# Attention followed by two feed-forward stages: another order for the start, the division by row sums through a wide copy, and 24 products of ones

## The chip, the cores and the metric

The kernel runs on one core of a Trainium2 chip. The metric is the device time of one execution in microseconds. The engines of the core are TensorE (PE; its weight loads are listed as PEld and overlap with its products), VectorE (DVE), ScalarE (ACT), GpSimd (POOL) and SyncE (SP), which issues the transfers. Each engine takes its own instructions in order, and an instruction that waits holds up all that stand behind it on that engine.

## The reference

```python
def _attn_ref(q, k, v, g_q, g_k):                  # 4 x 12 heads x 448 x 64
    def rmsnorm(x, g):
        rms = np.sqrt(np.mean(x * x, axis=-1, keepdims=True) + 1e-06)
        return x / rms * g
    q_n, k_n = (rmsnorm(q, g_q), rmsnorm(k, g_k))
    scores = np.matmul(q_n, k_n.transpose(0, 1, 3, 2)) / np.sqrt(64)
    scores = scores - np.max(scores, axis=-1, keepdims=True)
    attn = np.exp(scores)
    attn = attn / (np.sum(attn, axis=-1, keepdims=True) + 1e-09)
    return np.matmul(attn, v)
...
x = attn_out.transpose(0, 2, 1, 3).reshape(1792, 768)
h = x @ w_in                                       # 768 -> 2048
x = np.maximum(0.01 * h, h) @ w_out                # 2048 -> 768
...
for e in range(8):                                 # each token goes to its best expert
    h = np.maximum(x[mask] @ w1[e], 0.0)
    out[mask] = gate_w[mask, None] * eom[mask, e, None] * (h @ w2[e])
```

## The kernel before

The kernel has three stages: attention, a feed-forward stage (`FirstMoe`), and a second one with eight experts. The change is in the attention alone.

**Tiling.** The 48 heads are taken as 24 pairs (`PAIRS`). Both heads of a pair lie side by side on the 128 partitions, 64 each. The 448 rows of a head are NC = 4 chunks of CP = 112 rows.

**One pair, step by step.** `load` fetches q and k into `qk` (112 x 1024, L177), `load_v` fetches v (L183). `square` squares both on ACT (L192) and adds up each row's 64 squares on DVE (L193) into `ms`. `roots` makes the inverse root of `ms` in nine small DVE steps (L213 to L222); `together` lays the `ms` of two pairs side by side, so that one chain of roots serves both. `norm` multiplies q and k by it (L240, on POOL, for the first pair half on DVE). `turn_k` and `turn_q` transpose the normed chunks on PE (L248) and write them as a high part on ACT (`kh` L267, `qh` L256) and a low part on DVE (`kl` L268, `ql` L63). `top` makes the scores of one chunk (L275), and DVE takes their maximum per row (`md`, L277). `row` transposes the four maxima (L282), and ACT copies them to `mx` (L284). `probs` makes the scores again, transposed, from high and low parts with the maximum taken off (L298, eight products), and ACT takes exp of them (L300, `p` or `pr`). POOL adds the four chunks' exponentials into `pr` (L313). `values` multiplies them with v into `av` (L309).

**The division.** `sums` adds up the exponentials over the partitions with products against `ones_mat` (L321), ACT copies them to `sp` (L325), `back` turns them with four small products (L332), and DVE takes the reciprocals `r`, 112 x 8 (L335). `spread` lays them out in the shape of `av`: eight products of `r`, broadcast to 64 columns, with `ident` (L342; the trace counts 16, two for each float32 product). `scale` copies that to `rt` on ACT (L348) and multiplies `av` with it on DVE (L350). `store` writes the result as `xTh` (ACT, L355) and a low part (DVE, L63).

**The order.** In the attention the order on PE, DVE, ACT and POOL is as written out by hand in `pieces`: a prologue for pair 0, `begin(i)` for the pairs 0 to 2, `steady(i)` for the pairs 3 to 22. While pair i makes its `probs`, the next one (`one`) makes its tops and the one before (`prev`) is divided and stored. The last pair and `FirstMoe` are placed by a scheduler. From pair 8 on, weights of `FirstMoe` are fetched and unpacked beside the attention (`decode`, L580 to L588, on ACT, DVE and POOL), in every second pair, and in some late ones where the scheduler puts more. In PSUM the transposes share two buffers (`tr`), the scores of `probs` have one (`sc`), the tops one (`tp`), `av` two. `FirstMoe` makes its first products at L627 to L629 (`mo`).

## Time and profile before

| what | value |
|---|---|
| three runs, median | 1232.29 us |
| three runs, lowest and highest | 1229.84 and 1232.62 us |
| the profiled execution | 1230.19 us |
| its span in the profile | 1228.4 us |
| PE busy | 1158.2 us (94%) |
| DVE busy | 775.5 us (63%) |
| ACT busy | 500.3 us (41%) |
| POOL busy | 456.4 us (37%) |

The span is the time from the first to the last instruction; 1.8 us of the execution lie around it. The shares are means over three stages with different limits, so a change in one stage is read from the rows of that stage: how long an engine was idle before an instruction, and which engine released it. The attention with its handover to `FirstMoe` takes the first 322 us or so, `FirstMoe` ends near 870, and the experts take the rest.

### The profile page before, as it was taken

To read this page: it belongs to the slowest core of one execution; us is meant where nothing else is said; L and a number is where in the kernel's file an instruction comes from. 1 tells how busy PE (TensorE), PEld (TensorE's weight loads), DVE (VectorE), ACT (ScalarE), POOL (GpSimd) and SP (SyncE) were. 2 spreads that over 40 slices of the span, in tenths; PEclk is the share of its full clock that TensorE was granted. 3 is DMA by queue.
4 is the path that set the end of the run, shared out by engine and by line. 5 is a ranking of instruction groups with operands and counts; after the bars stand their busy time and mean duration, and the time that the engine had idled before them with its cause. 6 is when DMAs were issued, how large, how long until landed. Compare 5 with 4: busy or idle time off the path is not lost.

```text
span 1228.4 us, 19094 instructions
## 1 busy us (share of the span) xinstructions
PE 1158.2 (94%) x6988; PEld 930.8 (76%) x6988; DVE 775.5 (63%) x1326; ACT 500.3 (41%) x791; POOL 456.4 (37%) x301
## 2 busy tenths in 40 slices
PE   4899999989899899999999999999799999999997
PEld 2455555545568788888888889888598988998986
DVE  6777888876627786858585854446745179215446
ACT  2566666655335422222222321132344167225444
POOL 1667767757324331313232220000414047113334
PEclk9999999989899999999999999999699999999999
DMA  5212222111102220202020200343357059413456
GB/s 149 60 47 61 68 80 73 50 29 29 46 13 77 78 77 26 78 26 78 26 78 26 78 26 1 133 118 88 117 199 249 24 197 354 153 47 125 172 201 227
DMA packets 68081, 116.28 MB, mean 95 GB/s; under 512 B 6780, under 2 KB 45948, under 8 KB 67968
## 3 DMA queue, kind: packets, MB, share of 16 engines
q1 hardware_dynamic: 64528, 103.87, 26.6%
q0 software_dynamic: 3120, 11.02, 2.6%
q8 instruction: 57, 0.93, 0.3%
q14 instruction: 56, 0.46, 0.1%
q10 hardware_dynamic: 320, 0.00, 0.0%
HBM read 106.61 MB, written 12.58 MB: 97 GB/s over the span
## 4 chain that ended last, share of the span: by engine, by line
PE 77%; DVE 10%; issue 5%; ACT 3%; DMA 2%; POOL 2%; ACTq 0%; DVEq 0%; POOLq 0%; SPq 0%
PE mo L627 6%; PE mo L628 6%; PE mo L629 6%; PE sc L298 6%; PE av L309 6%; PE mp L646 6%; PE mp L647 5%; PE mp L648 5%; PE ph L990 4%; PE ph L989 3%; PE ph L988 3%; PE py L1006 3%; PE py L1004 3%; PE py L1005 3%; DVE w1l L63 2%
## 5 line engine op out<-in xcount | busy, mean ns | idle before, releaser
L654 DVE TENSOR_TENSOR ysum<-mp,ysum 128x448 f32<-128x448 f32 x168 | 103.8, 621 | 111.1 <-PE mp L648 109.5
L313 POOL TENSOR_TENSOR pr<-pr,p 112x896 f32<-112x896 f32 x72 | 153.2, 2128 | 49.6 <-ACT p L300 35.4
L627 PE MATMUL mo<-xTh,w0h 128*128 128x448 f32 x384 | 142.8, 372 | 13.2 <-DVE g L634 9.4
L646 PE MATMUL mp<-gh,w1h 128*128 128x448 f32 x384 | 144.4, 377 | 1.4 <-ACT ysum L652 0.7
L628 PE MATMUL mo<-xTl,w0h 128*128 128x448 f32 x384 | 141.8, 369 | 0.2 <-DVE xTl L63 0.2
L647 PE MATMUL mp<-gl,w1h 128*128 128x448 f32 x384 | 141.8, 369 | 0.0
L629 PE MATMUL mo<-xTh,w0l 128*128 128x448 f32 x384 | 141.4, 368 | 0.0
L648 PE MATMUL mp<-gh,w1l 128*128 128x448 f32 x384 | 140.4, 368 | 0.0
L588 POOL TENSOR_TENSOR raw<-raw,top 128x384 f32<-128x384 f32 x64 | 65.2, 1020 | 191.1 <-DVE raw L586 166.7
L277 DVE TENSOR_REDUCE md<-tp 112x2 f32<-112x896 f32 x96 | 104.4, 1088 | 17.7 <-PE tp L275 17.4
L1004 PE MATMUL py<-w2h,hT 128*128 128x384 f32 x288 | 99.7, 346 | 0.0
L63 POOL TENSOR_TENSOR w1l<-r,w1h 128x1024 fp32r<-128x1024 f32 x17 | 42.9, 2528 | 149.4 <-ACT w1h L952 75.1
L1006 PE MATMUL py<-w2l,hT 128*128 128x384 f32 x288 | 96.8, 336 | 0.0
L1005 PE MATMUL py<-w2h,hL 128*128 128x384 f32 x288 | 96.5, 335 | 0.0
L63 DVE TENSOR_TENSOR hL<-pt,hT 128x512 fp32r<-128x512 f32 x36 | 24.8, 689 | 106.3 <-ACTq L1014 59.3
L627 PEld LDWEIGHTS mo<-xTh,w0h 128*128 128x128 f32 x384 | 72.5, 189 | 24.1 <-DVE g L634 12.1
L990 PE MATMUL ph<-w1l,xgh 128*128 128x512 f32 x216 | 86.4, 400 | 4.2 <-DVE w1l L63 4.2
L988 PE MATMUL ph<-w1h,xgh 128*128 128x512 f32 x216 | 86.7, 402 | 0.0
L989 PE MATMUL ph<-w1h,xgl 128*128 128x512 f32 x216 | 85.8, 397 | 0.0
L63 POOL TENSOR_TENSOR w1l<-raw,w1h 128x768 fp32r<-128x768 f32 x16 | 31.4, 1984 | 141.7 <-ACT w1h L596 141.7
L646 PEld LDWEIGHTS mp<-gh,w1h 128*128 128x128 f32 x384 | 72.4, 189 | 13.0 <-DVE ysum L654 4.1
L300 ACT ACTIVATE p<-sc 112x896 f32<-112x896 f32 x72 | 66.0, 917 | 39.8 <-PE sc L298 35.6
(199 smaller groups left out, 2499.8 us busy)
## 6 DMA issues: line engine op xcount, KB each, us to landing
r<-in_moe_w_dram SPq DMA_DIRECT2D x27, 1024.0 KB, 5.5
r<-in_moe_w_dram SPq DMA_DIRECT2D x36, 768.0 KB, 7.3
wd<-in_moe_w_in_dram SPq DMA_DIRECT2D x32, 384.0 KB, 3.3
wd<-in_moe_w_out_dram SPq DMA_DIRECT2D x32, 384.0 KB, 3.1
qk<-in_q_dram SPq DMA_DIRECT2D x24, 224.0 KB, 3.0
qk<-in_k_dram SPq DMA_DIRECT2D x24, 224.0 KB, 3.2
vv<-in_v_dram SPq DMA_DIRECT2D x24, 224.0 KB, 2.8
x2d<-xn SPq DMA_DIRECT2D x24, 224.0 KB, 2.9
```

Of the source, the lines that this page charges most:

```text
L63: engine.tensor_tensor(dst, src, hi.bitcast(F32), ALU.subtract)
L313: nc.gpsimd.tensor_tensor(st["pr"][:CP], st["pr"][:CP], p, ALU.add)
L627: nc.tensor.matmul(ph, wh_[:, c], xh, start=(c == 0), stop=False)
L628: nc.tensor.matmul(ph, wh_[:, c], xl, start=False, stop=False)
L629: nc.tensor.matmul(ph, wl_[:, c], xh, start=False, stop=(c == KD - 1))
L646: nc.tensor.matmul(py, hi[:, sl], gh, start=(j == 0), stop=False)
L647: nc.tensor.matmul(py, hi[:, sl], gl, start=False, stop=False)
L648: nc.tensor.matmul(py, lo[:, sl], gh, start=False, stop=(j == GF - 1))
L990: nc.tensor.matmul(ph[n], xh[:, c], w1l[:, c, s_], start=False, stop=(c == K1 - 1))
L1004: nc.tensor.matmul(py[n], hT[:, c], w2h[:, c, s_], start=(c == 0), stop=False)
L1005: nc.tensor.matmul(py[n], hL[:, c], w2h[:, c, s_], start=False, stop=False)
L1006: nc.tensor.matmul(py[n], hT[:, c], w2l[:, c, s_], start=False, stop=(c == K2 - 1))
```

## The change

**Division.** A new step `widen` copies `r` on ACT to `wide` (112 x 512: each reciprocal 64 times). `spread` then transposes `wide` chunk by chunk, four transposes in place of eight float32 products. On PE `spread` moves from ahead of `probs` of chunk 3 to behind it, behind the next pair's first top and behind `row(one)`; `scale` moves with it. `square` is split, so that ACT squares before it widens and DVE's sum stands where it stood.

**Start.** The first two pairs are squared together, get one chain of roots (112 x 32), and pair 0 is normed wholly on DVE, k first, pair 1 on POOL. The transposes of pair 1 go in between the tops of pair 0, and these tops take turns between two buffers. The small product `gg` (L111, now `join_constants`) comes behind the sums of squares. One chain of roots moves from pair 0 to pair 1.

**Products of ones.** At the start PE makes WARM = 24 products of `ones_mat` with itself (128 x 128), which need no transfer, and ACT reads one column of the result (`seen`).

```diff
+    def join_constants():
         nc.vector.scalar_tensor_tensor(gg, gg, ROOT ** -2, gk, ALU.mult, ALU.mult)
...
-                (nc.vector if t and st is self.first else nc.gpsimd).tensor_tensor(
+                (nc.vector if st is self.first else nc.gpsimd).tensor_tensor(
...
-        def top(self, st, c):
-
-            sc = self.tp()
+        def top(self, st, c, other=0):
+
+            sc = self.sc() if other else self.tp()
...
+        def widen(self, st):
+
+            wide = self.pool.tile([CP, NC, 2, DH], F32, name="wide", bufs=1)
+            nc.scalar.activation(
+                wide, st["r"].rearrange("p j c -> p c j").unsqueeze(3).to_broadcast([CP, NC, 2, DH]), AF.Copy)
+            st["wide"] = wide
+
         def spread(self, st):
-            tr = st["tr"] = self.tr()
-            for c in range(NC):
-                for j in range(2):
-                    nc.tensor.matmul(
-                        tr[j * DH:(j + 1) * DH, c * CP:(c + 1) * CP],
-                        st["r"][:, j, c:c + 1].to_broadcast([CP, DH]), ident[:CP, :CP], start=True, stop=True)
+            st["tr"] = self.turned_of(st["wide"].rearrange("p c j d -> p c (j d)"))
...
-                st = sts[0]
-                self.together(sts[:1])
+                st, one = sts[:2]
+                self.together(sts[:2])
                 self.square(st)
-                self.roots(sts[:1])
-                self.norm(st)
+                self.square(one)
+                join_constants()
+                self.roots(sts[:2])
+                self.norm(st, (1, 0))
+                self.norm(one, (1, 0))
+                warm = self.sc()
+                for _ in range(WARM):
+                    nc.tensor.matmul(warm[:, 0, :P], ones_mat, ones_mat, start=True, stop=True)
+                seen = self.pool.tile([P, 1], F32, name="seen", bufs=1)
+                nc.scalar.activation(seen, warm[:, 0, :1], AF.Copy)
                 self.turn_k(st, 0)
                 self.turn_q(st, 0)
-                self.together(sts[1:2])
                 for c in range(NC):
-                    self.top(st, c)
+                    self.top(st, c, c % 2)
                     if c == 1:
-                        self.square(sts[1])
-                self.roots(sts[1:2])
+                        self.turn_k(one, 1, apart=True)
+                        self.turn_q(one, 1, apart=True)
                 self.row(st)
-                self.norm(sts[1])
+                one["klow"]()
+                one["low"]()
...
             self.back(prev)
+            if at(i + 6):
+                self.square(at(i + 6), (0,))
+            self.widen(prev)
             self.values(cur, 1)
-            self.spread(prev)
...
-            self.scale(prev)
             self.probs(cur, 3)
             if two:
                 self.top(two, 0)
+            self.row(one)
+            self.spread(prev)
             self.values(cur, 2)
+            self.scale(prev)
             self.store(prev)
-            self.row(one)
```

In the three places below a row is an instruction with its output, its inputs, its shape and its count.

PE at the start, before; `tr<-ident,qn` are the transposes of q and k, `md_137` the maxima of pair 0:

```order
L248 MATMUL tr<-ident,qn 128x112 x8
L275 MATMUL tp<-kh,qh 112x448 x8
L282 MATMUL tr<-ident,md_137 128x112 x4
L298 MATMUL sc<-qh,kh 112x448 x2
L298 MATMUL sc<-ql,kh 112x448 x2
```

PE at the start, after:

```order
L390 MATMUL sc<-ones_mat 128x128 x24
L254 MATMUL tr<-ident,qn 128x112 x8
L283 MATMUL tp<-kh,qh 112x448 x2
L283 MATMUL sc<-kh,qh 112x448 x2
L254 MATMUL tr<-ident,qn 128x112 x8
L283 MATMUL tp<-kh,qh 112x448 x2
L283 MATMUL sc<-kh,qh 112x448 x2
L290 MATMUL tr<-ident,md_137 128x112 x4
L306 MATMUL sc<-qh,kh 112x448 x2
L306 MATMUL sc<-ql,kh 112x448 x2
```

The ones come first, and the eight transposes of pair 1 now stand between the tops of pair 0 (in the kernel before they follow its first `probs`).

PE in a steady pair, before, from `back` to the next pair's first transposes:

```order
L332 MATMUL av<-ident,sp 112x4 x2
L309 MATMUL av<-p,vv 64x448 x2
L342 MATMUL tr<-ident,r 64x112 x8
L298 MATMUL sc<-qh,kh 112x448 x2
L298 MATMUL sc<-ql,kh 112x448 x2
L298 MATMUL sc<-qh,kl 112x448 x2
L298 MATMUL sc<-mx,mask 112x448 x2
L275 MATMUL tp<-kh,qh 112x448 x2
L309 MATMUL av<-p,vv 64x448 x2
L282 MATMUL tr<-ident,md_139 128x112 x4
L248 MATMUL tr<-ident,qn 128x112 x4
```

PE in the same steady pair, after:

```order
L340 MATMUL av<-ident,sp 112x4 x2
L317 MATMUL av<-p,vv 64x448 x2
L306 MATMUL sc<-qh,kh 112x448 x2
L306 MATMUL sc<-ql,kh 112x448 x2
L306 MATMUL sc<-qh,kl 112x448 x2
L306 MATMUL sc<-mx,mask 112x448 x2
L283 MATMUL tp<-kh,qh 112x448 x2
L290 MATMUL tr<-ident,md_139 128x112 x4
L254 MATMUL tr<-ident,wide 128x112 x4
L317 MATMUL av<-p,vv 64x448 x2
L254 MATMUL tr<-ident,qn 128x112 x4
```

The eight products on `r` are gone from their place, and four transposes of `wide` stand behind `probs`, top and row.

ACT in the same steady pair, before, from the exp of chunk 2 (the first row) to the next pair's first exp (the last):

```order
L300 ACTIVATE p<-sc 112x896
L192 ACTIVATE sq<-qk 112x1024
L348 ACTIVATE rt<-tr 128x448
L300 ACTIVATE p<-sc 112x896
L355 ACTIVATE xTh_114<-av 128x448
L284 ACTIVATE mx<-tr 128x448
L267 ACTIVATE kh<-tr,gg 128x448
L300 ACTIVATE pr_133<-sc 112x896
```

ACT in the same steady pair, after:

```order
L308 ACTIVATE p<-sc 112x896
L197 ACTIVATE sq<-qk 112x1024
L349 ACTIVATE wide<-r 112x512
L308 ACTIVATE p<-sc 112x896
L292 ACTIVATE mx<-tr 128x448
L358 ACTIVATE rt<-tr 128x448
L365 ACTIVATE xTh_114<-av 128x448
L273 ACTIVATE kh<-tr,gg 128x448
L308 ACTIVATE pr_133<-sc 112x896
```

The copy to `wide` stands ahead of the exp of chunk 3, and `rt` moved behind that exp.

## Rows read from the trace of the kernel before

**Rows 1.** Stretches: us from and to, length, each engine's busy time, TensorE's granted clock

```profile
core 0: us, PE busy (x) PEld busy (x) DVE busy (x) ACT busy (x) POOL busy (x), PEclk, DMA share, GB/s
69.00:257.00 188.00, 186.12 (x1633) 105.49 (x1630) 153.39 (x262) 122.70 (x182) 134.71 (x85) 1.00 0.21 61
257.00:322.00 65.00, 54.53 (x421) 29.63 (x422) 43.18 (x61) 28.85 (x44) 40.34 (x24) 0.89 0.12 34
367.00:870.00 503.00, 487.60 (x2554) 432.46 (x2552) 335.17 (x663) 149.86 (x265) 117.58 (x86) 0.99 0.22 64
```

**Rows 2.** Time line at the start: start, us, engine, line, operation, [idle before <-releaser]

```profile
4.14 0.31 SPq L177 DMA_DIRECT2D qk<-in_k_dram  x1
...
7.06 1.27 DVE L193 TENSOR_REDUCE ms<-sq 112x8 f32<-112x512 f32 x2
...
11.09 1.82 PE L248 MATMUL tr<-ident,qn 112*128 112x112 f32 x8 [11.09 <-DVE qn L240]
...
14.29 1.09 DVE L277 TENSOR_REDUCE md<-tp 112x2 f32<-112x896 f32 x1
```

**Rows 3.** The page's transfers: issues, KB each, median us from issue to landing

```profile
qk<-in_k_dram SPq DMA_DIRECT2D x24, 224.0 KB, 3.2
```

**Rows 4.** Time line, PE, first three pairs

```profile
21.37 0.45 PE L282 MATMUL tr<-ident,md 112*128 112x112 f32 x1 [0.44 <-DVE md L277]
...
25.24 1.76 PE L248 MATMUL tr<-ident,qn 112*128 112x112 f32 x8 [1.66 <-POOL qn L240]
...
37.61 0.32 PE L282 MATMUL tr<-ident,md 112*128 112x112 f32 x1 [0.58 <-DVE md L277]
...
55.12 0.67 PE L282 MATMUL tr<-ident,md 112*128 112x112 f32 x4
```

**Rows 5.** Time line, the roots and the stall of the second pair

```profile
38.72 1.03 DVE L213 TENSOR_SCALAR ms<-ms 112x32 f32<-112x32 f32 x1
...
39.85 2.08 DVE L214 TENSOR_SCALAR y<-ms 112x32 int32<-112x32 int32 x1
...
45.69 0.45 PE L275 MATMUL tp<-kh,qh 64*112 64x448 f32 x2 [3.42 <-DVE md L277]
```

**Rows 6.** Time line, PE in a steady pair

```profile
112.56 0.59 PE L321 MATMUL tr<-pr,ones_mat 113*32 113x112 f32 x16
...
115.66 0.99 PE L342 MATMUL tr<-ident,r 112*64 112x112 f32 x16
...
116.57 0.46 PE L298 MATMUL sc<-qh,kh 64*112 64x448 f32 x2
...
118.68 0.60 PE L282 MATMUL tr<-ident,md 112*128 112x112 f32 x4
...
119.12 0.55 PE L248 MATMUL tr<-ident,qn 112*128 112x112 f32 x4
...
124.33 0.59 PE L321 MATMUL tr<-pr,ones_mat 113*32 113x112 f32 x16
```

**Rows 7.** Groups by line and shape: count, busy us, mean ns, idle before

```profile
L192 ACT ACTIVATE sq<-qk 112x512 f32<-112x512 f32 x2 | 1.1, 612 | 0.0
```

**Rows 8.** Time line, ACT in the same steady pair

```profile
115.06 1.05 ACT L192 ACTIVATE sq<-qk 112x1024 f32<-112x1024 f32 x1
...
117.74 0.92 ACT L300 ACTIVATE p<-sc 112x896 f32<-112x896 f32 x1 [0.44 <-PE sc L298]
```

**Rows 9.** Time line, PE in the pair of the first late stall

```profile
262.72 1.76 PE L342 MATMUL tr<-ident,r 112*64 112x112 f32 x16 [3.97 <-DVE r L335]
...
269.21 0.46 PE L298 MATMUL sc<-qh,kh 64*112 64x448 f32 x2
```

**Rows 10.** Time line before the first feed-forward stage

```profile
304.30 1.74 DVE L581 TENSOR_SCALAR top<-wd 128x384 int32<-128x384 int32 x1 [2.31 <-DMA wd<-in_moe_w_out_dram]
...
310.34 0.71 PE L275 MATMUL tp<-kh,qh 64*112 64x448 f32 x2 [2.22 <-DVE md L277]
...
321.42 0.47 PE L627 MATMUL mo<-xTh,w0h 128*128 128x448 f32 x1 [1.86 <-DVE md L277]
```

More of the change, by code (lines that the diff above doesn't have):

```diff
@@ L184, in load_v, with square @@
                 st["v"], v[b, 2 * hp:2 * hp + 2].rearrange("h (p c) d -> p h (c d)", c=NC))
-        def square(self, st):
+        def square(self, st, parts=(0, 1)):
             n = 4 * NC
             flat = st["qk"].rearrange("p t h (c d) -> p (t h c) d", d=DH)
-            sq = self.early.tile([CP, n, DH], F32, name="sq", bufs=2)
+            if 0 in parts:
+                st["sq"] = self.early.tile([CP, n, DH], F32, name="sq", bufs=2)
+            sq = st["sq"]
             for h in (slice(0, n // 2), slice(n // 2, n)) if st is self.first else (slice(0, n),):
-                nc.scalar.activation(sq[:, h], flat[:, h], AF.Square, scale=DH ** -0.5)
-                nc.vector.tensor_reduce(st["ms"][:, h], sq[:, h], AX.X, ALU.add)
+                if 0 in parts:
+                    nc.scalar.activation(sq[:, h], flat[:, h], AF.Square, scale=DH ** -0.5)
+                if 1 in parts:
+                    nc.vector.tensor_reduce(st["ms"][:, h], sq[:, h], AX.X, ALU.add)
         def together(self, sts):
@@ L260, in turn_q, with turn_k @@
             st.update(qh=qh, ql=ql, md=self.MX[i % len(self.MX)], pr=self.PR[i % len(self.PR)])
-        def turn_k(self, st, i):
+        def turn_k(self, st, i, apart=False):
             kh = self.pool.tile([P, S], F32R, name="kh", bufs=3)
@@ L267, in turn_k @@
             nc.scalar.activation(kh, tk, AF.Copy, scale=gg)
-            nc.vector.scalar_tensor_tensor(kl, tk, gg, kh.bitcast(F32), ALU.mult, ALU.subtract)
+            st["klow"] = lambda: nc.vector.scalar_tensor_tensor(kl, tk, gg, kh.bitcast(F32), ALU.mult, ALU.subtract)
+            if not apart:
+                st["klow"]()
             st.update(kh=kh, kl=kl)
-        def top(self, st, c):
-            sc = self.tp()
+        def top(self, st, c, other=0):
+            sc = self.sc() if other else self.tp()
             for j, rows in enumerate(HALVES):
@@ L397, in pieces @@
                     self.back(sts[n - 2])
+                    self.widen(sts[n - 2])
                 elif op == "C":
@@ L406, in pieces @@
             self.back(last)
+            self.widen(last)
             yield
@@ L417, in begin @@
                 todo = [[("square", 2)], [("roots", 2, 3), ("norm", 2)], [("square", 3)],
-                        [("square", 4), ("roots", 3, 5)]]
+                        [("square", 4)]]
             elif i == 1:
-                todo = [[("norm", 3)], [("square", 5)], [("norm", 4)], []]
+                todo = [[("roots", 3, 5), ("norm", 3)], [("square", 5)], [("norm", 4)], []]
             else:
                 todo = [[("square", 6)], [("roots", 5, 7), ("norm", 5)], [("norm", 6)], []]
-            for lo, hi in {0: ((2, 3), (3, 5)), 1: ((5, 7),)}.get(i, ()):
+            for lo, hi in {0: ((3, 5),), 1: ((5, 7),)}.get(i, ()):
                 self.together(sts[lo:hi])
             for c in range(NC):
-                if c == 3 and prev:
-                    self.scale(prev)
                 self.probs(cur, c)
-                if i == 0 and c == 0:
-                    self.turn_k(one, 1)
-                    self.turn_q(one, 1)
                 self.top(one, c)
@@ L434, in begin @@
                     self.back(prev)
+                    self.widen(prev)
+                elif c == 3 and prev:
+                    self.spread(prev)
+                    self.scale(prev)
                 if c:
@@ L440, in begin @@
                     self.sums(prev)
-                elif c == 2 and prev:
-                    self.spread(prev)
                 elif c == 3 and prev:
@@ L503, in steady @@
             self.back(prev)
+            if at(i + 6):
+                self.square(at(i + 6), (0,))
+            self.widen(prev)
             self.values(cur, 1)
-            self.spread(prev)
             if not begun:
@@ L511, in steady @@
             if at(i + 6):
-                self.square(at(i + 6))
+                self.square(at(i + 6), (1,))
             yield
-            self.scale(prev)
             self.probs(cur, 3)
@@ L518, in steady @@
                 self.top(two, 0)
+            self.row(one)
+            self.spread(prev)
             self.values(cur, 2)
+            self.scale(prev)
             self.store(prev)
-            self.row(one)
             if three:
@@ L529, in attention_moe_moe2 @@
     FROM = 3
+    WARM = 24
     ORDER = "P0 S P1 C V0 P2 V1 P3 V2 V3".split()
```

1 line of the change is left out of this document (added).

## The prediction

> **What bounds the kernel now.** I read the busy times by stretch first, then the time line of the stretches in which TensorE is idle. In the steady attention TensorE works 186.1 of 188 us, and in the first feed-forward stage 487.6 of 503 [rows 1]. In both it is the bound: whatever else is made faster there gives nothing, and what is taken off TensorE comes back in full until another engine is late. VectorE, the next, has 153.4 of the 188. Between 257 and 322 TensorE works 54.5 of 65 us, at a granted clock of 0.89. There it waits, so the reader must look at what ends each wait. The start is the third kind: TensorE's first instruction comes at 11.09 [rows 2], and three marks divide what follows, the transposes of the maxima that close the prologue, the first and the second pair, at 21.37, 37.61 and 55.12 [rows 4]. These are 10.3, 16.2 and 17.5 us, while a steady pair takes 124.33 - 112.56 = 11.77 [rows 6].
>
> The clock at the start is read from durations: eight transposes take 1.82 at 11.09 and 1.76 at 25.24 [rows 2, 4], where four take 0.55 later on [rows 6], so TensorE is still at its lower level of 1.2 GHz, after a start in which it did nothing.
>
> **The steady pairs.** On TensorE the spread of the reciprocals takes from 115.66 to 116.57, 0.91 us. The transposes that replace it have the form of those at 118.68, which take 0.44 until the next begin [rows 6]. That is 0.47 less in each pair; I take 0.44, for a change of form between the products. ScalarE pays for it with one copy of 112x512. The nearest row is the square of that shape, 0.61 us [rows 7]; the copy reads a broadcast of 112x8, which no row shows, so I bound it by half of that and by the full 112x1024 square, 1.05 [rows 8], and take 0.61, the same output. It is hidden: the square ends at 116.11, r is out before 115.66 (where TensorE takes it now), so the copy ends near 116.7. The exp behind it starts now at 117.74; without the spread ahead of its products it could start at 116.8. TensorE comes to the new transposes only behind four more groups of products and one of transposes, near 118.6, so it doesn't wait for the copy. On ScalarE the copy to rt now stands between the exp and the next pair's kh, and the next exp, now at 120.70 and then wanted at 120.25, comes out within about 0.1 us of that: a tie, not a reserve. VectorE has (188 - 153.4)/188 of its time free, enough for a pair that is 4% shorter. There are 18 pairs from the 4th to the 23rd without a stall: 18 x 0.44 = 7.9, between 6 and 8.5.
>
> **The start.** The chain to the first transposes gets longer. The second pair's k is issued at 4.14 and needs 3.2 [rows 2, 3], so it is there at 7.3; a square of 1.05 [rows 8] ends at 8.4, its sums (two halves take 1.27, [rows 2]) at 9.6, where the sums now end at 8.33. From there to the first transposes it is 2.76 now, and the roots of twice the columns cost a little more (0.15, an estimate). First transposes: 11.09 + 1.3 + 0.15, about 12.5. From there the first maximum is taken 3.2 later now (11.09 to 14.29, at the lower clock). With two buffers for the tops the four maxima follow each other at 1.09, with one low part of about 0.7 before the row: 12.5 + 3.2 + 4 x 1.09 + 0.7 = 20.8, and 20.1 with a fast clock, against 21.37 now. The prologue gives about 0.9.
>
> The gain is behind it. The first pair then has no transposes of the second in it, and VectorE's four maxima, three sums of squares and two small chains set it: 4 x 1.09 + 3 x 1.27 + about 2, some 10.2 us; with TensorE's part at a lower clock up to 13. So its mark comes at 31 to 33.7 (37.61 now). In the second pair the stall of 3.42 at 45.69 goes [rows 5], with its roots one step earlier; but two root steps there took 1.03 and 2.08 us beside GpSimd's additions, more together than the whole chain and norm of pair 0 (2.76), and the changed kernel puts a chain of roots in the same pair. I take 12.9 for it, a steady pair and 1.1 of such delay. Its mark then comes at 44 to 46.6 instead of 55.12: 8.5 to 11. I take 9, near the slow end, because the clock may be slow again (below).
>
> What the Trainium skill says of this delay (SBUF — State Buffer, "SBUF: two separate sides") is that VectorE and GpSimd share a port pair as an exclusive lock, held for a whole instruction. The two rows agree in size with that, since a GpSimd addition lasts about as long as the longer of them. By the page the delay would come back wherever roots meet additions, which is what I assume.
>
> **The products of ones** are 24 with two passes each. Sixteen passes of 112 columns take 1.76 slow and 0.99 fast [rows 6, 9], so 48 of 128 columns take 6.0 or 3.4, and up to 10.6 if a pass costs what a transpose costs at the slow level (1.82 / 8, [rows 2]). They need no transfer, so they lie within the wait for the first transposes and cost nothing. They end between 5 and 12, so TensorE may be idle again for up to 7 us before it begins at 12.5. The rows tell what idling does: after 3.97 us the spread at 262.72 took 1.76 in place of 0.99 [rows 9]. So I count no gain in the first transposes themselves. The term above holds without the ones.
>
> **The late stalls.** In the pair around 262 TensorE stands 3.97 us for the reciprocals, because they queue on VectorE behind unpacking of weights, and then runs the spread, the products, and all up to 269.21 partly at the lower clock [rows 9]. In the new order the products of chunk 3, a top and the row stand ahead of the spread, so they run inside the wait. What is left behind r is the copy, the spread and one group of values: the next pair's products could begin at about 265.0 instead of 269.21, 4.2 with the 0.45 of a clean pair in it. The price of the move: the exp of chunk 3 now stands behind the copy, which waits for r, and the POOL additions behind that exp. I take 3.0, between 0.45 and 4.3.
>
> Between 297 and 322 VectorE waits for weights from memory (2.31 at 304.30), TensorE for VectorE (2.22 at 310.34, 1.86 at 321.42) [rows 10]. No edit makes those transfers earlier in themselves, but TensorE has more to do in the wait. I take 3.0, between 0 and 6. The last pair gets the copy in its chain and loses 0.47 on TensorE: nothing. Behind that the two feed-forward stages are unchanged and TensorE's, so what is gained ahead of them stays.
>
> **Sum.** 9 + 7.9 + 3.0 + 3.0 = 22.9 off the profiled execution's 1230.2 gives 1207.3. That execution lies 2.1 below the median of the three runs, 1232.3, from which the same sum gives 1209.4. I say 1208.
>
> **Rivals.**
> Slow clock at the start: the gap behind the ones returns TensorE to 1.2 GHz, and it stays there through the first pair, whose products then bound it. For it speaks the row at 262.72, against it that a pair without gaps came back within some 5 us there (at 269.21 a group takes 0.46 again). The start then gives 5 or 6 instead of 9: 1212. The Trainium skill (TensorE: Matmul & The Clock Gate, "Part 4: PE-mode transpose") adds that transposes don't count as busy for the clock in the same way as products; by it the sixteen transposes of the new prologue would prolong this. The row at 25.24, slow after 14 us of transposes and tops, doesn't speak against it.
>
> The stalls stay: VectorE is as late for weights as before, and the exp behind the copy makes the GpSimd additions, and with them the sums, late. Then the last two terms give 0.9 instead of 6: 1213.
>
> The tie on ScalarE is lost: each pair's next exp comes 0.4 late and takes the saving of the steady pairs. The sum is 15 instead of 22.9: 1216.
>
> Slower than before: the broadcast copy is far dearer than a square of its shape. The exp behind it must be over when the next pair's products need their buffer, near 119.1, so start by 118.2; from 116.11 the copy may take 2.1 us without harm. Past that each microsecond costs one in each of some 21 pairs. The gain of 22.9 and 3.7 more, over 21 pairs, is 1.3: from 3.4 us on the kernel is slower by more than 0.3%, and at 4.0 it takes about 1247 (1207.3 + 21 x 1.9). For it speaks only that no row shows such a read; against it the 0.61 of the same output.
>
> That the change doesn't do what it says holds for the ones: if they end early, the first transposes take 1.8 as before. It costs nothing in my sum.
>
> **Chances and range.** My forecast 0.62, slow clock 0.15, stalls that stay 0.12, the lost tie 0.06, the dear copy 0.05, of which 0.02 within 0.3% of before (3.7 us, what a measurement of this kernel can tell from none) and 0.03 beyond. All but the last are faster: 0.95. The range runs from the upper ends of the terms (11 + 8.5 + 4.3 + 6 = 29.8, 1200 to 1202; I cut it to 1200, since they will hardly all come together) to the lost tie, 1216.
>
> **What will show it.** The first transposes near 12.5, and their duration, 1.8 or 1.0; the transposes of the maxima near 20.5, 32.5 and 45.5; four transposes of the wide tile in 0.44, a steady period of 11.3 us, and the copy at 0.6 with no wait of an exp behind it; in the pair of 262 no long wait for r on TensorE with work queued behind; the first product of the feed-forward stage near 298.5. I am wrong if the steady period stays at 11.7, if the second mark comes after 35, or if the wait before the first feed-forward product grows by what was gained ahead of it.

## The result, and the profile after

The changed kernel takes 1214.5 us (median of four runs, 1211.78 to 1217.62) where the kernel before takes 1232.39: a ratio of 0.986, with a 95% interval of 0.9833 to 0.9887, or 17.9 us less. The profiled execution took 1211.78 with a span of 1210.0, the shortest of the four; against the 1228.4 of before that is 18.4. The forecast was 1208, with a range of 1200 to 1216.

The place of the gain is read from marks in both time lines: the start of the sums of a pair (the 16 products with `ones_mat`, L321 before and L329 after), the first product of `FirstMoe`, the start of its last `mp` product (L646 before, L668 after), and the end.

| mark | before | after | earlier by |
|---|---|---|---|
| sums of the 4th pair | 89.02 | 81.30 | 7.7 |
| sums of the 18th pair | 255.29 | 242.87 | 12.4 |
| sums of the 19th pair (first late stall) | 273.96 | 259.31 | 14.65 |
| sums of the 21st pair | 297.49 | 282.09 | 15.4 |
| first product of `FirstMoe` | 321.42 | 303.71 | 17.7 |
| last `mp` product | 860.4 | 841.8 | 18.6 |
| end | 1228.4 | 1210.0 | 18.4 |

So the four terms of the sum came out as 7.7 for the start (9 forecast), 5.45 for the steady pairs (7.9; 4.70 up to the 18th pair and 0.75 in two more), 2.2 for the first late stall (3.0) and 2.3 for the handover to `FirstMoe` (3.0). The other 0.7 appears only behind the first product of `FirstMoe`.

The steady pair that answers to [rows 6] and [rows 8], after, on TensorE and ScalarE:

```profile
115.49 0.59 PE L329 MATMUL tr<-pr,ones_mat 113*32 113x112 f32 x16
...
117.99 1.05 ACT L197 ACTIVATE sq<-qk 112x1024 f32<-112x1024 f32 x1
118.33 0.20 DVE L343 RECIPROCAL r<-av 112x8 f32<-112x8 f32 x1
...
118.94 0.62 ACT L349 ACTIVATE wide<-r 112x512 f32<-112x512 f32 x1
...
119.75 0.92 ACT L308 ACTIVATE p<-sc 112x896 f32<-112x896 f32 x1 [0.20 <-PE sc L306]
...
120.22 0.55 PE L254 MATMUL tr<-ident,wide 112*128 112x112 f32 x4
...
120.70 0.97 PE L317 MATMUL av<-p,vv 112*64 112x448 f32 x4
...
121.60 0.60 PE L254 MATMUL tr<-ident,qn 112*128 112x112 f32 x4
...
122.14 0.46 PE L306 MATMUL sc<-qh,kh 64*112 64x448 f32 x2
...
123.25 0.92 ACT L308 ACTIVATE pr<-sc 112x896 f32<-112x896 f32 x1
...
126.88 0.59 PE L329 MATMUL tr<-pr,ones_mat 113*32 113x112 f32 x16
```

From sums to sums it is 11.39 instead of 11.77. The transposes of `wide` run from 120.22 to 120.70, 0.48 where the eight products took 0.91, without a wait; the copy ends at 119.56, and the exp behind it waits only for its products. But the transposes of `qn`, which stood right behind other transposes, now stand behind products and hold TensorE from 121.60 to 122.14, 0.54 where it was 0.48. 0.91 - 0.48 - 0.06 = 0.37, and 0.38 is measured.

The start, after, answering to [rows 2] and [rows 4]:

```profile
1.14 8.12 PE L390 MATMUL sc<-ones_mat 128*128 128x128 f32 x48 [1.14 <-DVE ones_mat L70]
...
8.46 1.06 ACT L197 ACTIVATE sq<-qk 112x1024 f32<-112x1024 f32 x1 [2.27 <-DMA qk<-in_k_dram]
...
12.81 2.14 DVE L246 TENSOR_TENSOR qn<-qk,y 112x512 f32<-112x512 f32 x2
12.86 2.99 POOL L246 TENSOR_TENSOR qn<-qk,y 112x512 f32<-112x512 f32 x2 [10.01 <-DVE y L228]
13.65 0.98 PE L254 MATMUL tr<-ident,qn 112*128 112x112 f32 x4 [4.40 <-DVE qn L246]
...
22.93 0.98 PE L290 MATMUL tr<-ident,md 112*128 112x112 f32 x4 [2.50 <-DVE kl L274]
...
35.72 0.32 PE L290 MATMUL tr<-ident,md 112*128 112x112 f32 x1 [0.57 <-DVE md L285]
...
47.89 0.60 PE L290 MATMUL tr<-ident,md 112*128 112x112 f32 x4
```

The three marks of the prediction are at 22.93, 35.72 and 47.89. The second pair's k, issued at 4.02, is there at 8.46, 4.4 us later. In the trace of before, where it is issued at 4.14, the transfer takes longer than the median of all 24 in [rows 3], too:

```profile
qk<-in_k_dram SPq DMA_DIRECT2D x1, 224.0 KB, 4.8
```

The ones end at 9.26. TensorE then stands idle for 4.40 us, and its first transposes take 0.98 for four: the clock is at its lower level again. The granted clock (the third number from the right in the rows by stretch) says so for the 16 us behind it:

```profile
0.00:9.00 9.00, 7.87 (x48) 7.87 (x48) 5.00 (x20) 3.16 (x5) 2.19 (x14) 1.00 0.73 192
9.00:14.00 5.00, 0.60 (x5) 0.44 (x4) 4.14 (x13) 0.57 (x2) 1.14 (x1) 0.92 1.13 238
14.00:30.00 16.00, 11.85 (x52) 6.94 (x50) 10.93 (x13) 5.68 (x8) 1.85 (x2) 0.50 0.49 105
30.00:34.00 4.00, 4.00 (x28) 1.98 (x28) 3.12 (x12) 2.22 (x3) 2.13 (x3) 0.97 0.00 0
```

The two late stalls are 16.44 and 15.67 us from sums to sums, where they were 18.67 and 18.89.

### The profile page after: what moved, and what is told of

The parts are those of the page before. It is cut to its first block, busy times and chain, and to the rows that moved or that the text cites. A ratio compares the mean times of both kernels' runs of the same rounds, so it can differ in the third digit from the quotient of the medians.

```text
span 1210.0 us, 18647 instructions
## 1 busy us (share of the span) xinstructions
PE 1153.1 (95%) x6748; PEld 927.2 (77%) x6748; DVE 775.3 (64%) x1318; ACT 509.8 (42%) x816; POOL 454.1 (38%) x300
## 4 chain that ended last, share of the span: by engine, by line
PE 71%; DVE 15%; issue 4%; ACT 4%; DMA 2%; POOL 2%; ACTq 0%; DVEq 0%; SPq 0%; POOLq 0%
PE mo L649 6%; PE mo L650 6%; PE mo L651 6%; PE mp L668 5%; PE mp L669 5%; PE mp L670 5%; PE sc L306 5%; PE av L317 4%; PE ph L1012 3%; PE ph L1011 3%; PE ph L1010 3%; PE py L1028 3%; PE py L1026 3%; PE py L1027 3%; DVE w1l L63 2%
## 5 line engine op out<-in xcount | busy, mean ns | idle before, releaser
L321 POOL TENSOR_TENSOR pr<-pr,p 112x896 f32<-112x896 f32 x72 | 151.9, 2109 | 31.2 <-ACT p L308 17.4
L649 PE MATMUL mo<-xTh,w0h 128*128 128x448 f32 x384 | 143.2, 373 | 11.4 <-DVE g L656 9.5
L668 PE MATMUL mp<-gh,w1h 128*128 128x448 f32 x384 | 144.3, 377 | 2.2 <-DVE ysum L676 1.1
L285 DVE TENSOR_REDUCE md<-tp 112x2 f32<-112x896 f32 x94 | 102.2, 1087 | 18.5 <-PE tp L283 17.9
L649 PEld LDWEIGHTS mo<-xTh,w0h 128*128 128x128 f32 x384 | 72.5, 189 | 22.9 <-DVE g L656 12.9
L668 PEld LDWEIGHTS mp<-gh,w1h 128*128 128x128 f32 x384 | 72.4, 189 | 14.0 <-DVE ysum L676 4.1
```

What stands on the lines that cost most here:

```text
L321: nc.gpsimd.tensor_tensor(st["pr"][:CP], st["pr"][:CP], p, ALU.add)
L649: nc.tensor.matmul(ph, wh_[:, c], xh, start=(c == 0), stop=False)
L668: nc.tensor.matmul(py, hi[:, sl], gh, start=(j == 0), stop=False)
```

## The experiments

Twelve kernels ran, all on the kernel after except `div`, which is the kernel before with the new division. Each is described below. The profiled marks of those that move the early attention (us; "late stall" is the time from the sums of the 18th pair to those of the 19th; the last line is the median of the runs):

| | before | after | div | start | here | move | noones | ones38 | port | fill | start2 |
|---|---|---|---|---|---|---|---|---|---|---|---|
| first transposes | 11.09 | 13.65 | 11.10 | 13.6 | 13.2 | 13.5 | 14.00 | 13.78 | 14.24 | 14.80 | 12.54 |
| sums, 4th pair | 89.02 | 81.30 | 88.79 | 82.96 | 87.96 | 81.23 | 82.28 | 81.88 | 81.09 | 80.39 | 77.27 |
| sums, 18th pair | 255.29 | 242.87 | 250.24 | 249.17 | 263.40 | 248.22 | 243.80 | 243.47 | 242.76 | 241.97 | 238.96 |
| late stall | 18.67 | 16.44 | 14.91 | 19.03 | 18.76 | 16.59 | 17.35 | 17.75 | 16.47 | 17.74 | 17.68 |
| first of `FirstMoe` | 321.42 | 303.71 | 310.0 | 315.4 | 330.0 | 313.7 | 306.3 | 305.9 | 304.2 | 304.3 | 302.4 |
| end | 1228.4 | 1210.0 | 1219.2 | 1225.8 | 1241.0 | 1222.0 | 1213.4 | 1214.6 | 1211.2 | 1212.9 | 1211.1 |
| median of runs | 1232.4 | 1214.5 | 1222.5 | 1227.4 | 1242.6 | 1224.4 | 1215.2 | 1215.8 | 1213.7 | 1214.0 | 1212.8 |

**div, the new division alone.** The start of before; copy, transposes and new places as in the changed kernel.

```diff
+    def widen(self, st): ...
     def spread(self, st):
+        st["tr"] = self.turned_of(st["wide"].rearrange("p c j d -> p c (j d)"))
...
```

> The start of the kernel before, with the wide copy, the four transposes and their later place. Theory: the parts add up, and the steady pairs, the late stall and the handover gave 5.5 + 2.2 + 3.2 us: about 1219 in a profiled run, the steady pair 11.39, the marks of the first pairs as before. Rival: the late gains hang on when the weights land, so that without the earlier start they differ; then the total lies outside 1216 to 1222 while the steady pair still takes 11.39.

The steady pair is 11.37 to 11.41, and the ratio to before 0.9929 (0.9906 to 0.9953): 8.7 us. Up to the first product of `FirstMoe` it is 11.4. The late stall is 14.91, less than in the changed kernel; its waits are the same, and the clock is not (below, under the late stall). The median lies half a microsecond beyond the bound that I set for the theory; where that went is below, with `start`.

**start, the new start alone.** The changed kernel with the eight products on `r` in their old place, without the copy.

```diff
-        st["tr"] = self.turned_of(st["wide"].rearrange("p c j d -> p c (j d)"))
+        tr = st["tr"] = self.tr()
+        ...                       # eight products of r with ident, ahead of probs of chunk 3
```

> The start and the products of ones of the changed kernel, with the eight products on r in their old place. Theory: gives the start's 7.7 alone, about 1222.5; steady pair 11.77; the stall near 260 with its wait of about 4 us as before. Rival: the 3 us of the handover come from the earlier start (weights and attention in another phase), then 1219 or less.

The start gives 6.1 and not 7.7 at the fourth pair's sums: the other 1.7 comes from the new division, which stands in the early pairs too (with the old start, in `div`, it gives only 0.2 there). It is the new place that gives it: `move`, which has the old form there, comes at 81.23. The stall stays (19.03). At the first product of `FirstMoe` the two halves add up: 11.4 + 6.0 = 17.4, where the whole change has 17.7. At the end they don't: 8.7 + 3.9 is 12.6 by the medians (ratio of `start` 0.997, 0.9956 to 0.9984), where the whole has 17.9. By the 95% intervals the whole gives 13.9 to 20.6 and the halves 5.8 to 11.6 and 2.0 to 5.4, so noise can be a part of that. In the profiled executions the difference is in `FirstMoe`. From its first product to its last it takes 539.0 before, 538.1 after, 540.9 in `div` and 542.3 in `start`.

The stage itself is as before, but the last three divisions still stand behind its first product, as 12 transposes of `wide` (after and `div`) or as 48 products on `r` (before and `start`), and the difference comes where they stand. Behind the 31st of VectorE's 168 running sums of the second products (`ysum`), which is 184 to 188 us in, all kernels here take 354.2 to 354.6 to the last product. Up to it, the changed kernel, `div` and `start`:

```profile
303.70:487.30 183.60, 173.58 (x859) 148.02 (x860) 121.30 (x205) 68.40 (x122) 59.95 (x42) 0.98 0.20 56
310.00:496.40 186.40, 175.66 (x859) 149.97 (x860) 119.08 (x205) 68.16 (x122) 60.51 (x42) 0.96 0.19 56
315.40:503.10 187.70, 176.87 (x906) 150.41 (x907) 119.99 (x207) 66.44 (x119) 60.50 (x43) 0.98 0.19 55
```

Most of it is busy time of TensorE: in `div` 2.1 of 2.8 us for the same instructions, at a lower granted clock (0.96), in `start` 3.3 of 4.1 with the products on `r`. The rows on what TensorE waits for, of the changed kernel (347 to 842) and then of `start` (361 to 858; `g` are the activated first products):

```profile
PE mo L649 <- DVE g L656: 9.5, 7, 4.2
PE mp L668 <- DVE ysum L676: 1.1, 1, 1.1
PE mp L668 <- ACT ysum L674: 0.7, 2, 0.4
```

```profile
PE mo L652 <- DVE g L659: 7.1, 7, 1.7
PE mp L671 <- ACT ysum L677: 3.7, 5, 1.4
PE mp L671 <- DVE ysum L679: 1.9, 1, 1.9
```

The waits for the running sum grow from 1.8 to 5.6, and those for `g` fall from 9.5 to 7.1 (the numbers are us in total, times, and the longest). Over all kernels here the stretch from first to last product is 537.9 to 542.8 long. Each length is that of one execution, and the executions of the changed kernel alone spread by 5.8 us. What sets clock and waits there is left open.

**here, the new form in the old place.**

```diff
             self.widen(prev)
             self.values(cur, 1)
+            self.spread(prev)
             ...
+            self.scale(prev)
             self.probs(cur, 3)
-            self.row(one)
-            self.spread(prev)
```

> The changed kernel with the wide copy and the four transposes, but these stand where the eight products stood, ahead of the products of chunk 3. Theory: TensorE then waits for square and copy (about 1.0 us from the place where it took r), so the steady pair is 11.77 - 0.43 + 1.0, about 12.3, and the total near 1233. Rival: the gain is the cheaper form and the place does nothing: steady pair 11.4 and total about 1217.

```profile
PE tr L254 <- ACT wide L349: 10.9, 13, 0.9
```

That is TensorE's only wait for another engine's data of any size between 92 and 250: 13 times, 0.84 each, for the copy. The steady pair is 12.42, and the kernel is slower than before, 1.0081 (1.0061 to 1.0102). The form alone loses 15 us against `start`; the place makes it a gain. It is 9.6 slower than I expected: `start` itself is 4.9 above what I had worked out for it, and the 2nd to 4th pairs pay too (5 us more than `start` at the fourth pair's sums).

**move, the old form in the new place.**

```diff
-        st["tr"] = self.turned_of(st["wide"].rearrange("p c j d -> p c (j d)"))
+        ...                       # eight products of r, behind probs, top and row; no copy
```

> The changed kernel with the eight products on r in place of copy and transposes, but in the new place behind products, top and row. Theory: the place alone takes nothing off a steady pair (11.77, perhaps 0.06 more for the change of form) and keeps the gain in the late stalls: about 1218 to 1220. Rival: the stalls are shorter because of the copy's place on ScalarE or because of the shorter pairs; then the stall near 260 takes its 18.7 again and the total is 1222 or more.

The steady pair is 11.77 and 12.21 where weights are unpacked (12.06 before), so the place alone takes nothing off it. The late stall is 16.59, as in the changed kernel: it is the place that shortens the stall, not the copy. The median, 1224.4, is 3.0 below `start` and 4 above what I expected. The handover gives nothing here: 9.0 us ahead of before at the sums of the 21st pair, 7.7 at the first product of `FirstMoe`, where the changed kernel goes from 15.4 to 17.7 and `div` from 9.5 to 11.4. That gain needs the new form too. And `FirstMoe` takes 540.4, 1.4 longer than before.

**noones and ones38, no products of ones, and 38.** The first cut is of `noones`, the second of `ones38`.

```diff
-                for _ in range(WARM):
-                    nc.tensor.matmul(warm[:, 0, :P], ones_mat, ones_mat, start=True, stop=True)
...
-    WARM = 24
+    WARM = 38
```

> The changed kernel without the 24 products of ones and the column that ScalarE reads. Theory: the ones end 4.4 us before the first transposes, the clock falls back, so they give nothing: marks of the first pairs within 0.5 us of the changed kernel's, total within 1. Rival: they spare the first pairs part of the slow clock; then the sums of the first pair come 1 to 3 us later and so does the end.

> 38 products of ones in place of 24. The second half of the 24 took 0.27 us each, so 38 end near 13.1, right ahead of the first transposes at 13.65. Theory: the first transposes then run at the upper level (0.55 in place of 0.98), tops and products too, and the second mark comes 2 to 3 us earlier: total 2 to 3 lower. Rival: VectorE sets the prologue and the first pair whatever the clock, then less than 1.

Without ones the median is 1215.15 (1215.07 to 1215.66), within the spread of the changed kernel. The landing of the second pair's k moves the first transposes by some tenths from run to run, so I compare what lies between them and the sums of the fourth pair: 67.65 after, 68.28 without ones, 68.10 with 38. But `split` (below), whose instructions up to there are those of the changed kernel, ones included, took 68.26. So a spread of 0.6 is there without any edit, and neither the 24 nor the 38 are shown to be worth anything. With 38 the first transposes do run fast, but the clock falls behind them, as the granted clock of the same stretch shows, first of `ones38`, then of `fill` (below):

```profile
14.00:30.00 16.00, 11.44 (x52) 6.51 (x50) 11.28 (x14) 5.68 (x8) 1.99 (x2) 0.55 0.39 98
```

```profile
14.00:30.00 16.00, 14.52 (x112) 10.56 (x112) 12.65 (x18) 6.62 (x11) 2.99 (x2) 1.00 0.41 105
```

**fill, ones in every gap of the prologue.**

```diff
+                def fill(m):
+                    for _ in range(m):
+                        nc.tensor.matmul(spare[:, :P], ones_mat, ones_mat, start=True, stop=True)
                 self.turn_k(st, 0)
+                fill(4)
                 self.turn_q(st, 0)
+                fill(4)
...
+                fill(12)
                 self.row(st)
...
+    WARM = 44
```

> The changed kernel with products of ones wherever TensorE stands idle up to the first pair: 44 ahead of the first transposes, then 4, 4, 3 and 12 between the transposes and tops of the prologue (into a spare buffer of av). Theory: the clock fell in the changed kernel because TensorE stood still, or worked only by transposes, between 9.3 and 23; with products in every gap it stays at the upper level, the first pair's products take 0.37 in place of 0.58, its mark comes about 2 us earlier (near 33.7) and the end 1.5 to 2.5. Rival: VectorE sets the first pair all the same (its mark moves by under 0.7), or the ones hold up the prologue.

The clock holds at 1.00, the first pair's products take 0.37, and from the first mark to the second it is 10.7 us (23.42 to 34.16) where it was 12.8. From the first transposes to the sums of the fourth pair it is 65.59, 2.1 less than in the changed kernel and 2.7 less than in `split`. This kernel's first transposes came 1.15 later (14.80), and the late stall took 17.74 in place of 16.44, so at the first product of `FirstMoe` nothing is left: 304.3 against 303.7. The theory on the clock holds; the end doesn't show it.

The Trainium skill (TensorE: Matmul & The Clock Gate, "Part 4: PE-mode transpose") states that transposes don't count as busy for the clock as products do. `ones38`, whose gap ahead of the transposes was under 2 us, agrees in that its clock fell while TensorE did transposes and little else; but it had idle time between them too, so no run here tells the two apart.

**port, the norms one behind the other.**

```diff
                 self.norm(st, (1, 0))
+                yone = self.pool.tile([CP, 4 * NC], F32, name="yone", bufs=1)
+                nc.vector.tensor_copy(yone, one["yf"])
+                one["yf"] = yone
                 self.norm(one, (1, 0))
```

> The changed kernel with one more small copy on VectorE (112x16) behind the two norms of pair 0, from which GpSimd's norms of pair 1 read, so that they start only then. Theory: the two norms on VectorE took 2.14 together because GpSimd's two ran beside them; alone they take 1.4, the first pair's second transposes come 0.6 us earlier, and the marks and the end move by 0.3 to 0.7. Rival: their time is their own; no change, or 0.2 later for the copy.

```profile
13.40 1.29 DVE L246 TENSOR_TENSOR qn<-qk,y 112x512 f32<-112x512 f32 x2
14.61 0.17 DVE L388 COPY yone<-y 112x16 f32<-112x16 f32 x1
14.86 2.04 POOL L246 TENSOR_TENSOR qn<-qk,yone 112x512 f32<-112x512 f32 x2 [12.01 <-DVE yone L388]
```

VectorE's two norms take 1.29 in place of 2.14. From their start to the prologue's mark it is 9.49 where it was 10.12, and from the first transposes to the sums of the fourth pair 66.85 where it was 67.65. `best` (below), with the same start, bears out the first (8.44 us from the first transposes to the prologue's mark, 8.65 in `port`, 9.28 after), but not the second: 67.52, for the spread named above. At the end the medians, 1213.74 and 1214.5, can't be told apart.

**wide4, the copy four times.**

```diff
+            for _ in range(3):
+                nc.scalar.activation(wide, ..., AF.Copy)
```

> The changed kernel with the wide copy made four times over: 2.5 us of ScalarE in place of 0.62 in each pair. Theory: the copy has about 2.1 us from the square's end before the exp behind it holds up the next pair's products, so a steady pair grows by 0.4 to 0.7 and the total by 8 to 15. Rival: ScalarE has more room (no change), or none at all (each 1.9 comes through: about 40).

```profile
133.21 0.62 ACT L349 ACTIVATE wide<-r 112x512 f32<-112x512 f32 x1
...
133.86 1.95 ACT L352 ACTIVATE wide<-r 112x512 f32<-112x512 f32 x3
...
135.72 0.90 ACT L308 ACTIVATE p<-sc 112x896 f32<-112x896 f32 x1
135.86 0.60 PE L254 MATMUL tr<-ident,wide 112*128 112x112 f32 x4 [1.11 <-ACT wide L352]
```

A pair grows by 1.43, not by 0.4 to 0.7, and the kernel is slower than before: 1.0164 (1.0145 to 1.0183). The median is 36.5 above the changed kernel's where I expected 8 to 15, near the rival without any room (about 40); 10 of it lie ahead of the sums of the fourth pair. It is not the exp's consumer that waits first, as I had worked out, but the transposes themselves, 1.11 us, for the last copy. Of the 1.9 us added, 0.5 was room.

**split and best, unpacking in two parts.** `split` moves the last three of five unpacking steps on VectorE, and GpSimd's one, behind the next maximum; `best` adds `port`.

```diff
             if two:
                 two["low"]()
+            self.more()           # the last three steps of the unpacking begun in this pair
```

> The changed kernel with the last three steps of unpacking on VectorE (and GpSimd's one) moved behind the next maximum and the low part. Theory: the pairs that unpack take 11.81 in place of 11.39 because that maximum stands behind all five steps; with two ahead of it they take 11.4 to 11.5: five such pairs before the late stall, 1.5 to 2 us, and the late stall as before or shorter. Rival: VectorE's total work sets these pairs, then 11.8 stays.

> The changed kernel with both: GpSimd's norms of pair 1 behind VectorE's of pair 0, and unpacking in two parts. Theory: the gains add, 0.6 and 1.5 to 2, so 2 to 2.6 us less than the changed kernel, if the late stall does not take some of it back. Rival: the wait for weights takes it back, and the total is within 1 us of the changed kernel's.

The pairs that unpack take 11.40 as expected, but the pairs behind them 13.0 to 14.6 in place of 11.39, and the medians are 1223.24 and 1222.32. The rows of one of those pairs:

```profile
134.26 4.31 POOL L321 TENSOR_TENSOR pr<-pr,p 112x896 f32<-112x896 f32 x2
...
137.34 1.27 DVE L219 TENSOR_SCALAR ms<-ms 112x32 f32<-112x32 f32 x1
...
138.53 1.04 POOL L246 TENSOR_TENSOR qn<-qk,y 112x512 f32<-112x512 f32 x1
138.71 0.89 DVE L220 TENSOR_SCALAR y<-ms 112x32 int32<-112x32 int32 x1
...
141.11 1.08 DVE L285 TENSOR_REDUCE md<-tp 112x2 f32<-112x896 f32 x1
...
142.25 0.46 PE L283 MATMUL tp<-kh,qh 64*112 64x448 f32 x2 [1.39 <-DVE md L285]
```

GpSimd's addition came later, so all its work did, and the roots on VectorE now meet it: two steps of 0.2 take 1.27 and 0.89, each up to the end of the GpSimd instruction beside it (138.61 and 138.57, 139.60 and 139.57), the maximum behind them is late, and TensorE waits 1.39. That is what [rows 5] showed for the second pair. The Trainium skill (SBUF — State Buffer, "SBUF: two separate sides") gives a shared port pair of these two engines as an exclusive lock; `port` and `split` agree, with 0.85 and 1.8 us.

**start2, three things at the start.** `fill` (38, 1, 4, 3 and 12) and `port`, and v of the first pair fetched behind q and k of the second.

```diff
-    att.load_v(att.first)
...
+                fetch(2)
+                self.load_v(self.first)
                 fetch(3)
```

> The changed kernel with three things at the start: v of the first pair is fetched behind q and k of the second; GpSimd's norms of pair 1 wait for VectorE's of pair 0; products of ones fill TensorE's gaps (38, then 1, 4, 3 and 12). Theory: the square of pair 1 starts near 6.8 in place of 8.46, so the first transposes come near 12.4 in place of 13.65; the separate norms give 0.6 behind that and the clock 2, together about 3.5 to 4 at the sums of the fourth pair (81.3 before); the rest as in the changed kernel, so 2.5 to 4 at the end, the late stall's spread of some 1.5 included. Rival: another limit takes it back in the first pair (VectorE's four maxima and three sums of squares take 8 to 10 us whatever stands ahead), then under 2.

The sums of the fourth pair come at 77.27, 4.0 earlier than in the changed kernel, as expected, and 3.9 of it is still there at the 18th. The late stalls then take 17.68 and 17.00 in place of 16.44 and 15.67, and `FirstMoe` is 2.2 longer. The median is 1212.8 (1211.72 to 1214.26), the ratio to before 0.9841 (0.9823 to 0.9859): of the 4 us, 1.7 are left by the medians and none by the profiled executions (spans of 1211.1 and 1210.0), within the spread of the changed kernel's runs. It is the fastest that ran, but no proven gain on the changed kernel.

**What sets the late stall.** Its two waits are the same, within 0.1 us, in the changed kernel, `div`, `noones`, `ones38`, `port`, `fill` and `start2`. Two units of weights are unpacked in this pair. The second one's transfer is issued when the first is done with the one buffer, and VectorE waits for it with the maxima and `r` behind it in its queue. After, and in `div`:

```profile
243.62 0.35 SPq L580 DMA_DIRECT2D wd<-in_moe_w_out_dram  x1
...
246.98 0.92 DVE L603 TENSOR_SCALAR top<-wd 128x384 int32<-128x384 int32 x1 [1.91 <-DMA wd<-in_moe_w_out_dram]
...
248.95 0.45 PE L283 MATMUL tp<-kh,qh 64*112 64x448 f32 x2 [1.50 <-DVE md L285]
...
251.09 0.60 PE L254 MATMUL tr<-ident,wide 112*128 112x112 f32 x4 [1.15 <-ACT wide L349]
251.22 1.08 DVE L285 TENSOR_REDUCE md<-tp 112x2 f32<-112x896 f32 x1
251.62 1.29 PE L317 MATMUL av<-p,vv 112*64 112x448 f32 x4
```

```profile
256.32 0.45 PE L279 MATMUL tp<-kh,qh 64*112 64x448 f32 x2 [1.50 <-DVE md L281]
256.70 0.60 PE L286 MATMUL tr<-ident,md 112*128 112x112 f32 x4
...
258.45 0.60 PE L252 MATMUL tr<-ident,wide 112*128 112x112 f32 x4 [1.15 <-ACT wide L345]
258.98 0.97 PE L313 MATMUL av<-p,vv 112*64 112x448 f32 x4
```

TensorE waits 1.50 and 1.15, in `start2` 1.50 and 1.14. What differs is the clock behind the waits. In `div` it stays (values in 0.97, granted clock 1.00 from 259 to 263) and the pair takes 14.91; after it falls at about 251.7 and comes back at about 255.4, and the pair takes 16.44; in `start2` it is down already for the transposes (1.01 in place of 0.60), 0.50 from 248 to 252, and the pair takes 17.68. The same work and the same waits cost 2.8 us more or less by that. No run shows why the clock falls in one and not in the other.

## Why the prediction was right, and where its terms were off

- **The total.** It lies in the range, near its slow end: the terms added up to 22.9, and 17.9 is measured. All four came out smaller than forecast, and the width of the range covers that.
- **The bound.** It holds in part. TensorE set the steady pairs and `FirstMoe`, and what the changed kernel gained ahead of `FirstMoe` (17.7) was there at its end (18.4). "What is gained ahead of them stays" is not a rule, though: `div` lost 2.2 of its 11.4 and `start` 3.4 of its 6.0, most of it in the first part of `FirstMoe`. The kernels with the division of the changed kernel took 537.9 to 540.9 from first to last product there, and its own 538.1 is near the short end: that it lost nothing is in part luck.
- **The steady pairs, 7.9 forecast, 5.45 measured.** The mechanism was right and hidden as worked out; three sizes were off. The saving of a pair is 0.38, not 0.44 (the `qn` transposes lose their neighbour). In the five pairs that unpack it is 0.25: the maximum of the next top stands behind five steps on VectorE, that time is not TensorE's, and the wait for it takes back a third of what was saved (these pairs take 0.29 more than the others before, 0.42 now). And there were 16 such pairs between the marks, not 18.
- **The place.** "TensorE doesn't wait for the copy" held in the steady pairs only because the transposes were moved: `here` is slower than before. The reserve was mis-sized, though. I gave the copy 2.1 us before it harms; `wide4` shows 0.62 + 0.5, about 1.1, and the transposes wait before the exp's consumer does. The rival of the dear copy would have begun at a third less than I said: (18.4 + 3.7) / 21 + 1.1, some 2.2 us, or 2.0 with the 36.5 us that `wide4` lost for its 1.43 a pair (both estimates). The copy cost 0.62, as taken from the row of the square.
- **The tie on ScalarE** did no harm: the next pair's exp, now at 123.25, stands 0.41 behind the start of its last products (122.84), as before (120.70 and 120.30), and nothing else holds it up.
- **The start, 9 forecast, 7.7 measured**, of which 6.1 are the start's own and 1.7 come from the division in the first pairs, which I had not counted there. A sign of being wrong that I had named came true: the second mark stands at 35.72, after 35. The three marks were forecast near 20.5, 32.5 and 45.5 and came at 22.93, 35.72 and 47.89. The step that failed is "the prologue gives about 0.9": its mark is 1.56 later than before (21.37). The gain lies behind it, 3.45 us in the first pair (12.79 in place of 16.24) and 5.34 in the second (12.17 in place of 17.51, the stall of 3.42 gone). The first transposes came at 13.65, not 12.5: k of the second pair was there at 8.46, not 7.3, so its sums were done at 10.8, not 9.6. I had priced that transfer at the median of 24, 3.2, where the trace of before has 4.8 for this one. From the first transposes to the mark it was 9.28 where I had 8.3. The second norm on VectorE came 0.7 late, because GpSimd's norms ran beside it. I had priced that contention for the roots of the second pair and not for the norms; there (one root step of 0.83 in place of 1.03 and 2.08) it was smaller than I took.
- **The slow clock** was a rival at 0.15 with 1212 us, and the clock did fall behind the ones and stay low for 16 us. That mechanism came true, with `fill` putting its price at 2.1 to 2.7 us where I had 3 to 4. The number 1212 is near the profiled run's for another reason: some two thirds of what is missing from my sum ahead of `FirstMoe` (3.2 of 5.2) lies in the steady pairs and the stall.
- **The late stalls, 3.0 and 3.0 forecast, 2.2 and 2.3 measured.** The products did run inside the wait, and `move` shows that in the first stall the place does it. The step that failed is "products of chunk 3, a top and the row stand ahead of the spread, so they run inside the wait": the top itself waits 1.50, for a maximum in the same queue of VectorE. With the clock up (`div`) the gain is 3.8, with the 0.4 of the cheaper form in it; with the clock down 0.9 to 2.2.
- **The products of ones** cost nothing and gave nothing that stands out of the spread. They took 8.12 us, within the 6.0 to 10.6 that I gave them (48 passes at 1.82 / 8 are 10.9, not 10.6; nothing hangs on it).

Open: what sets the clock and the waits in the first 184 to 188 us of `FirstMoe`, where nearly all of its difference arises (537.9 to 542.8 us), and why the clock falls in one late stall and not in another.

## What to carry to other kernels

A cheaper operand that needs one more step on another engine (here a copy on ScalarE) is a gain only where the waiting engine has other work to put ahead of it; try form and place apart: here the form alone lost 15 us, the place alone gave 3.0, and the form on top of it 9.9. Price a transfer at the start by its own landing, not by the median over the kernel. Where a stall is ended by a shared queue, look for every instruction that waits on that queue before you count work as running inside the stall. Products that keep TensorE's clock up have to reach the work that needs it: ones that end microseconds ahead gave nothing that can be told from the spread, ones in the gaps as well 2.1 to 2.7 us, and a gain far ahead of a stall can be lost again there.

## What the runs showed of the hardware

- The same two waits of TensorE (1.50 and 1.15 us with about 1.0 us of work between them) left the clock up in one kernel (`div`, granted 1.00) and let it fall in others (0.50 from 248 to 252 in `start2`); the pair's time changed from 14.91 to 17.68.
- Two VectorE multiplications of 112x512 took 2.14 us beside the same two on GpSimd and 1.29 alone; GpSimd's two took 2.04 alone (`port`) and 2.99 beside VectorE's. A root step of 0.17 to 0.19 us took up to 2.08 beside GpSimd's additions [rows 5], and in `split` two of them ended within 0.04 us of the GpSimd instruction beside them.
- The granted clock's column reads 1.00 from 14 to 30 us in `noones`, and at the start of before, though the products there take 0.57: without an earlier change of level in the trace, durations have to tell the level.
- ScalarE's copy of eight reciprocals per row to 512 columns took 0.62 us, the time of a square of that size.
- Four float32 transposes hold TensorE for 0.48 us behind others of their kind and for 0.54 behind products with v.
